# Attention and MLP in one kernel: transposes of the last four half groups moved to DMA, loads two half groups ahead, a new plan

## The chip, the cores and the metric

The kernel runs on one core of a Trainium2 chip. The metric is the device time of one execution in microseconds (us), lower is better. Engines are called as the profile calls them: PE (TensorE matmul), PEld (its weight load), DVE (VectorE), ACT (ScalarE), POOL (GpSimd), SP (SyncE, which here only issues DMAs). A trailing q (SPq) is the part of an engine that issues DMAs and waits.

## What is computed

Inputs are q, k, v and f_logit, each 4 batches x 8 heads x 768 positions x 48, and two MLP weights, 384 x 2048 and 2048 x 384, all float32. Cut to what matters:

```python
f = 1.0 / (1.0 + np.exp(-f_logit))
for t in range(S):
    state = f[:, :, t, :, None] * state + np.einsum('bhd,bhe->bhde', k[:, :, t], v[:, :, t])
    y[:, :, t] = np.einsum('bhd,bhde->bhe', q[:, :, t], state)
x = y.transpose(0, 2, 1, 3).reshape(B * S, H * D)     # 3072 x 384
h = x @ w_in
out = (h * (1.0 / (1.0 + np.exp(-h)))) @ w_out        # 3072 x 384
```

So there is a linear attention with a decay per channel, and then an MLP with a SiLU over every row of its result.

## The kernel before, in words

**Tiling.** Positions go in chunks of 128, so there are six chunks; batches go in two halves of two. A *half group* m (0 to 11) is one chunk of one half; j (0 or 1) is the batch in it. A unit (m, j) is 128 positions of one batch with its 8 heads. m = 0 is loaded and computed in a special way (WIDE), the others alike.

**Tasks.** The work is cut into named tasks; "A8.0" is task A of m = 8, j = 0. For a unit, in the order of their dependence:

- f, k, q, v: the four loads, 192 KB each, issued by SP (load, L250).
- L (ACT): exp and ln of the gate; cs (PE, L314): cumulative sum; ia, aa (ACT): exponentials of it; al, ea: the chunk's total decay.
- ki (POOL, L327) and qg (DVE, L330): k and q scaled by them, in bf16, 64 columns for each head. vb (POOL): v in bf16.
- T (PE, transposes, L363): q and k are turned, eight 128x128 matmuls against an identity into PSUM; qk (DVE, L368) copies them to SBUF.
- A (PE, scores, L386): k times q; am (DVE, masked, L397): causal mask; Y (PE, outputs, L416 and L420): the unit's result; yc (DVE, L435): copied to SBUF in bf16; D and st: the state for m + 2.
- X (PE, turn, L441): three 128x128 transposes of y; xT (DVE, turned, L446) copies them to SBUF.

The MLP of a half group follows: I (PE) multiplies xT by w_in, S (ACT) does the SiLU into hT, O (PE) multiplies hT by w_out, R (ACT, L524) copies the result from PSUM, G stores it. Each is cut in steps: I of a half group has 8 steps of six 128x256 matmuls (mlp_in, L504), or, for m in SPLIT, 8 steps of twelve 128x128 ones (mlp_in_unit, L489), four for each j, so that they can start when one j is there; O has 8 steps of four 128x384 matmuls (mlp_out, L519). A step is named by its first index: I8.4, O7.1.12.

**What sets the order.** Every engine works its instructions in the program's order. A planner (class Plan) makes that order at build time: each task has an engine, an assumed duration, needs, a rank and the buffers that it takes; the planner plays the engines forward with these assumptions and always starts the task that can start first, the lower rank at a tie. MLP steps have ranks from 1000 up, so that attention goes first wherever it is ready. A need on another engine counts as done some time after its end (DRAIN: 0.24 for PE, 2.0 for a load), and for PE tasks of m >= 3 another 0.8 is added (spare), in the planner's units of a us. Where PE would have nothing, fillers (warm, L535: a matmul of zeros) are put in. The planner's durations are assumptions and no measurement; on the chip each engine simply waits at an instruction whose input isn't there.

**Loads.** The pool of load buffers has 8 for each of f, k, q, v, that is four half groups; the load of m waits until the task that reads the buffer of m - 4 is done. All loads, and the stores of m >= 8 (LATE), are issued by SP, in one order.

Of the kernel before, what the change touches and what calls it, by code (L numbers as in the profile page):

```python
# [11 lines left out]
F32 = mybir.dt.float32  # L12
# [6 lines left out]
class Plan:  # L19
# [14 lines left out]
    def add(self, name, engine, us, emit=None, needs=(), rank=0.0, takes=None, frees=None, table=None, opens=0,  # L34
            silus=0):

        m = int(name.lstrip(string.ascii_letters).split(".")[0] or 0)
        spare = self.spare if engine == "PE" and m >= 3 else 0.0
        self.tasks[name] = dict(name=name, engine=engine, us=us, emit=emit, needs=list(needs), rank=rank,
                                takes=[takes] if isinstance(takes, str) else takes or [], frees=frees, table=table, opens=opens, silus=silus, spare=spare)  # L40

    def transfers(self):

        queues = [[n for n, t in self.tasks.items() if t["engine"] == e] for e in ("LD", "WT")]
        left = {n: self.tasks[n]["us"] for q in queues for n in q}
        now = 0.0
        self.lands = {}
        while any(queues):
            heads = [q[0] if q and self.issued[q[0]] <= now else None for q in queues]
            if not any(heads):  # L50
                now = min(self.issued[q[0]] for q in queues if q)
                continue
            rates = self.SHARE if all(heads) else [1.0 if h else 0.0 for h in heads]
            step = min(left[h] / r for h, r in zip(heads, rates) if h)
            later = [self.issued[q[0]] - now for q, h in zip(queues, heads) if q and not h]
            step = min([step] + later)
            now += step
            for q, h, r in zip(queues, heads, rates):
                if h:
                    left[h] -= step * r  # L60
                    if left[h] < 1e-6:
                        self.lands[h] = now
                        q.pop(0)
# [14 lines left out]
    def run(self, filler=None):  # L78
# [6 lines left out]
        left = dict(tasks)  # L85
        for t in tasks.values():
            for n in t["needs"]:
                assert n in tasks, (t["name"], n)
        self.silus = self.ins = self.exps = turned = 0
        while left:  # L90
            best = None
            fronts = {}
            for t in left.values():
                ready = 0.0
                for n in t["needs"]:
                    if n not in end:
                        ready = None
                        break
                    ready = max(ready, end[n] + (self.DRAIN.get(tasks[n]["engine"], 0.1) + t["spare"]) * (tasks[n]["engine"] != t["engine"]))
                if ready is None:  # L100
                    continue
                p = self.pool_ready(t, end)
                if p is None:
                    continue
                e = t["engine"]
                start = max(ready, p, free.get(e, 0.0))
                swap = t["table"] is not None and table is not None and t["table"] != table
                fronts.setdefault(e, []).append((start, swap, t))
            for e, cands in fronts.items():
                cands = [c for c in cands if self.allowed(c, fronts, free)]  # L110
                if not cands:
                    continue
                first = min(s for s, _, _ in cands)
                now = [c for c in cands if c[0] <= first + 1e-6]
                choice = min(now, key=lambda c: c[2]["rank"])
                if best is None or choice[0] < best[0]:
                    best = choice
# [8 lines left out]
            if e in ("LD", "WT"):  # L126

                self.issued[t["name"]] = start
                free[e] = start
                end[t["name"]] = max(start + t["us"], self.lands.get(t["name"], 0.0))  # L130
                self.log.append((start, end[t["name"]], e, t["name"]))
                if t["emit"] is not None:
                    self.order.append((start, t["emit"]))
                del left[t["name"]]
                continue
# [33 lines left out]
            del left[t["name"]]  # L169
# [21 lines left out]
    spare = 0.8  # L191

# [6 lines left out]
def kernel(  # L199
# [10 lines left out]
    nc = tc.nc  # L210
# [7 lines left out]
    NT = d_ff // 128  # L218
    HB = B // 2
# [4 lines left out]
    ld = ctx.enter_context(tc.tile_pool(name="ld", bufs=8))  # L224
# [5 lines left out]

    WIDE = (0,)
# [22 lines left out]
    qg = [singles.tile([C, HB, H, 64], BF16, name=f"qg{i}") for i in range(4)]  # L254
    ki = [singles.tile([C, HB, H, 64], BF16, name=f"ki{i}") for i in range(4)]
# [102 lines left out]

    def transposes(m, j):
        t = tps.tile([128, 2, NP, C], BF16, name="t_ps")  # L360
        for i, src in ((0, qg), (1, ki)):
            for p in range(NP):
                nc.tensor.transpose(t[:, i, p, :], src[m % 4][:, j, 2 * p:2 * p + 2, :], ident)  # L363
        t_ps[m, j] = t

    def transposed(m, j):
        qkT[m, j] = wk.tile([128, 2, NP, C], BF16, name="qk", bufs=3)
        nc.vector.tensor_copy(qkT[m, j], t_ps[m, j])  # L368
# [56 lines left out]
    def output_copy(m, j):  # L425
        if m in WIDE:
            if j == 0:
                both = wk.tile([C, HB, HD], BF16, name="yw")
                for a in range(2):
                    ysb[m, a] = both[:, a]  # L430
                ysb[m] = both
# [83 lines left out]
    def mlp_out(m, j, n):  # L515
        if n == 0:
            os[m, j] = hps.tile([C, d_model], F32, name="o_ps", tag="h_ps")
        for i in range(n, n + 4):
            nc.tensor.matmul(os[m, j], hT[m][:, i, j * C:(j + 1) * C], w_out_sb[:, i, :],  # L519
                             start=(i == 0), stop=(i == NT - 1))  # L520

    def result(m, j):
        osb[m, j] = wk.tile([C, d_model], F32, name="o_sb", bufs=4)
        nc.scalar.copy(osb[m, j], os[m, j])  # L524

    def store(m, j):
# [3 lines left out]
        eng.dma_start(out=out[r0:r0 + C, :], in_=osb[m, j])  # L530
# [8 lines left out]
    plan = Plan({"yd": 2, "t": 1, "a": 1, "h": 3, "qk": 3, "atm": 2, "y": 2, "ia": 4, "aa": 4,  # L539
# [3 lines left out]
    def do(fn, *args):  # L543
# [3 lines left out]
    W = dict(m=8, j=3, L=0, cs=0, ia=-15, aa=1, ki=4, qg=1, vb=-8, T=7, qk=1, A=7, am=-2, Y=11,  # L547
             yc=1, D=25, st=-3, X=4, xT=-9, al=-4, ea=3, va=13)
    LATE = 8
    SPLIT = (1, 2, 3)  # L550
# [6 lines left out]
    for m in range(NH):  # L557
        for j, name in [(j, x) for x in "fkqv" for j in range(HB)] if m in WIDE else [(j, x) for j in range(HB) for x in "fkqv"]:
            user = U({"f": "L", "k": "ki", "q": "qg", "v": "vb"}[name], m - 4, j)
            first = (m, j, name) == (0, 0, "f")  # L560
            add(U(name, m, j), "LD", (0.85 if m in WIDE else 1.07) + 1.5 * first,
                None if m in WIDE else do(load, m, j, name), [user] if m >= 5 else [])

    add("issues", "ACT", 4.5, None, rank=-1e9)
    for m in range(NH):
# [3 lines left out]
        for j in range(HB):  # L569
# [16 lines left out]
            if wide:  # L586
# [3 lines left out]
            add(n("T"), "PE", 0.45, do(transposes, m, j), [n("qg"), n("ki")], rank=base + W["T"], takes="t")  # L590
            add(n("qk"), "DVE", 0.7, do(transposed, m, j), [n("T")], rank=base + W["qk"], takes="qk", frees=[n("T")])
            add(n("A"), "PE", 0.34, do(scores, m, j), [n("qk")], rank=base + W["A"], takes="a")
            add(n("am"), "DVE", 1.32, do(masked, m, j), [n("A")], rank=base + W["am"], takes="atm", frees=[n("A")])
            add(n("Y"), "PE", 0.45 if wide else 0.38, do(outputs, m, j), [n("am"), n("vb")] + ([n("va")] if wide else []) + olds,
                rank=base + W["Y"], takes="yd", frees=[n("qk"), n("am")])
# [5 lines left out]
            add(n("X"), "PE", 0.17, do(turn, m, j), ins("yc"), rank=base + W["X"], takes="yd", frees=[] if wide else [n("yc")])  # L601
            add(n("xT"), "DVE", 0.38, do(turned, m, j), [n("X")], rank=base + W["xT"], frees=[n("X")], takes="xT" if j == 0 else None)

        if m in SPLIT:
            for j in range(HB):
                for n in range(0, NT, 4):
                    add(f"I{m}.{j}.{n}", "PE", 0.68, do(mlp_in_unit, m, j, n),
                        [U("xT", m, j), f"wi{n // 4 * 512}"] + ([f"I{m}.{j}.{n - 4}"] if n else []),
                        rank=1000 + m * 10 + j * 3 + n * 0.1, takes=["h", "hT"] if j + n == 0 else "h", silus=4 if n == 0 else 0,
                        frees=[U("xT", m, 0)] if n == NT - 4 and j == HB - 1 else None)  # L610
                    add(f"S{m}.{j}.{n}", "ACT", 0.64, do(silu_unit, m, j, n), [f"I{m}.{j}.{n}"], rank=-1000 + m,
                        table="silu", frees=[f"I{m}.{j}.{n}"])
        else:
            for n in range(0, NT, 2):
                add(f"I{m}.{n}", "PE", 0.655, do(mlp_in, m, n),
                    [U("xT", m, j) for j in range(HB)] + [f"wi{n // 4 * 512}"] + ([f"I{m}.{n - 2}"] if n else []),
                    rank=1000 + m * 10 + n * 0.1, takes=["h", "hT"] if n == 0 else "h", silus=8 if n == 0 else 0,
                    frees=[U("xT", m, 0)] if n == NT - 2 else None)
# [3 lines left out]
        for j in range(HB):  # L622
            for n in range(0, NT, 4):
                add(f"O{m}.{j}.{n}", "PE", 0.655, do(mlp_out, m, j, n),
                    [f"S{m}.{j}.{n}" if m in SPLIT else f"S{m}.{n + 2}", f"wo{n}"] + ([f"O{m}.{j}.{n - 4}"] if n else []),
                    rank=1000 + m * 10 + 5 + j + n * 0.1, takes="h" if n == 0 else None,
                    frees=[owner] if n == NT - 4 and j == HB - 1 else None)
            add(f"R{m}.{j}", "ACT", 0.5, do(result, m, j), [f"O{m}.{j}.{NT - 4}"], rank=-500.0, frees=[f"O{m}.{j}.0"])
            add(f"G{m}.{j}", *(("SP", 0.05) if m >= LATE else ("POOL", 0.85)), do(store, m, j), [f"R{m}.{j}"], rank=-501.0)
            add(f"W{m}.{j}", "DMA", 0.6, None, [f"G{m}.{j}"], rank=-1)  # L630
# [71 lines left out]
```

## Time and profile before

| what | us |
|---|---|
| median of 6 runs (195.17 to 197.25) | 196.48 |
| the profiled execution, own time | 195.17 |
| its span, first to last instruction | 193.4 |
| PE busy | 186.6 |
| of it fillers (L535, 75 of them) | 16.1 |
| DVE, ACT, POOL busy | 111.6, 130.3, 56.9 |
| ACT table loads (14 of 1283 ns) | 18.0 |
| PE busy from 36.0 to 190.2 (154.2 us) | 153.8 |

The page's busy time of PE is from issue to end of pipelined matmuls, so that neighbours overlap; what a group costs PE is read from the distance of starts in the timeline. The idle time of an engine that is not on the chain is no loss.

### The profile page before, as it was taken

The page shows a single profiled execution, that of the slowest core. Times are in us where ns is not written, and L with a number is a line of the kernel's source. Part 1 is how long each engine was busy: PE and PEld are TensorE (multiplying, and loading weights), DVE is VectorE, ACT ScalarE, POOL GpSimd, SP SyncE. Part 2 cuts the span into 40 slices and gives each one's busy share as a digit, 9 for nine tenths or more (in the row PEclk, how much of TensorE's full clock was granted, in tenths as well). Part 3 has the DMA queues.
Part 4 walks back from the last instruction along what each step waited for, and adds up shares of the span by engine and source line. Part 5 has one row for each costly group of instructions (what it writes and reads, how often), then busy time and mean ns, then how long its engine had stood idle before and what let it go on. Part 6 is the DMA issues. An engine that isn't in the chain of part 4 may idle for free.

```text
span 193.4 us, 5153 instructions
## 1 busy us (share of the span) xinstructions
PE 186.6 (96%) x2127; PEld 141.1 (73%) x2127; DVE 111.6 (58%) x222; ACT 130.3 (67%) x244; POOL 56.9 (29%) x84
## 2 busy tenths in 40 slices
PE   7889999999999999999999999999999999999993
PEld 3457677998666687878688688976688679886561
DVE  6088875651057993877378989726887883000000
ACT  2764567678865489898989995799775027993111
POOL 7253990010367334241562332007720000000000
PEclk9999999999999999999999999999999999999999
DMA  4998999999999999999989897301120020000222
GB/s 110 222 205 176 184 195 191 184 185 176 215 228 259 208 214 196 218 208 211 218 214 217 179 247 164 69 0 41 51 75 3 0 81 3 0 3 0 81 81 81
DMA packets 101654, 27.06 MB, mean 140 GB/s; under 512 B 96256, under 2 KB 100864, under 8 KB 101632
## 3 DMA queue, kind: packets, MB, share of 16 engines
q1 hardware_dynamic: 94784, 19.67, 51.5%
q0 software_dynamic: 4736, 6.29, 14.5%
q10 hardware_dynamic: 2112, 0.79, 2.2%
q8 instruction: 16, 0.26, 0.6%
q14 instruction: 6, 0.05, 0.1%
HBM read 25.17 MB, written 4.72 MB: 155 GB/s over the span
## 4 chain that ended last, share of the span: by engine, by line
PE 61%; SPq 24%; DMA 9%; ACT 2%; issue 1%; ACTq 0%
SPq L250 24%; PE o_ps L519 24%; PE h_ps L504 22%; DMA f_ld<-in_f_logit_dram 7%; PE t_ps L363 3%; DMA f_w<-in_f_logit_dram 2%; PE a_ps L386 2%; PE h_ps L489 2%; PE y_ps L416 2%; PE y_ps L420 1%; PE x_ps L441 1%; PE d_ps L460 1%; PE cs L314 1%; PE al_ps L351 1%; ACT L287 1%
## 5 line engine op out<-in xcount | busy, mean ns | idle before, releaser
L519 PE MATMUL o_ps<-w_out_sb,hT 128*128 128x384 bf16 x384 | 68.6, 326 | 0.0
L504 PE MATMUL h_ps<-xT,w_in_sb 128*128 128x256 bf16 x432 | 52.1, 273 | 0.4 <-DMA w_in_sb<-in_moe_w_in_dram 0.4
L519 PEld LDWEIGHTS <-hT 128*128 128x128 bf16 x384 | 36.2, 98 | 21.3
L513 ACT ACTIVATE hT<-h_ps 128x512 bf16<-128x512 f32 x72 | 42.5, 597 | 12.0 <-PE h_ps L504 9.5
L504 PEld LDWEIGHTS <-w_in_sb 128*128 128x128 bf16 x432 | 40.5, 98 | 5.8 <-DMA w_in_sb<-in_moe_w_in_dram 0.6
L397 DVE TENSOR_TENSOR atm<-a_ps,triu 128x512 bf16<-128x512 f32 x44 | 28.3, 686 | 4.3 <-PE a_ps L386 4.1
L327 POOL TENSOR_TENSOR ki<-k_ld,ia 128x384 bf16<-128x384 f32 x22 | 22.6, 1032 | 24.0 <-ACT ia L319 21.3
L330 DVE TENSOR_TENSOR qg<-q_ld,a 128x384 bf16<-128x384 f32 x22 | 18.4, 843 | 19.2 <-ACT a L324 19.0
L524 ACT COPY o_sb<-o_ps 128x384 f32<-128x384 f32 x24 | 11.5, 477 | 23.5 <-PE o_ps L519 23.3
L336 POOL CAST vb<-v_ld 128x384 bf16<-128x384 f32 x22 | 12.5, 570 | 46.9 <-DMA v_ld<-in_v_dram 38.1
L368 DVE COPY qk<-t_ps 128x1024 bf16<-128x1024 bf16 x24 | 16.5, 686 | 5.7 <-PE t_ps L363 5.6
L287 ACT ACT_TABLE_LOAD x14 | 18.0, 1283 | 1.8 <-PEq L686 1.6
L489 PE MATMUL h_ps<-xT,w_in_sb 128*128 128x128 bf16 x288 | 18.5, 219 | 0.3 <-ACT hT L497 0.3
L435 DVE CAST y<-y_ps 128x384 bf16<-128x384 f32 x22 | 12.2, 554 | 9.5 <-PE y_ps L420 9.5
L489 PEld LDWEIGHTS <-w_in_sb 128*128 128x128 bf16 x288 | 16.6, 98 | 1.0 <-issue 0.4
L535 PE MATMUL w_ps<-zeros 128*128 128x384 bf16 x75 | 16.1, 360 | 1.2 <-DVE zeros L643 1.2
L497 ACT ACTIVATE hT<-h_ps 128x512 bf16<-128x512 f32 x24 | 13.8, 597 | 3.5 <-PE h_ps L489 2.8
L301 ACT ACTIVATE f_ld<-f_ld 128x384 f32<-128x384 f32 x22 | 11.6, 525 | 5.6 <-DMA f_ld<-in_f_logit_dram 5.5
L319 ACT ACTIVATE ia<-cs 128x384 f32<-128x384 f32 x24 | 11.5, 486 | 4.2 <-PE cs L314 3.5
L535 PEld LDWEIGHTS <-zeros 128*128 128x128 bf16 x75 | 7.7, 106 | 6.4 <-issue 2.2
L480 DVE TENSOR_TENSOR states<-sd,al 48x192 bf16<-48x192 f32 x32 | 11.8, 369 | 0.8
L530 POOL DMA_DIRECT2D out_dram<-o_sb x16 | 9.3, 582 | 9.3 <-ACT o_sb L524 6.6
(76 smaller groups left out, 201.4 us busy)
## 6 DMA issues: line engine op xcount, KB each, us to landing
f_ld<-in_f_logit_dram SPq DMA_DIRECT2D x22, 192.0 KB, 4.5
k_ld<-in_k_dram SPq DMA_DIRECT2D x22, 192.0 KB, 4.5
q_ld<-in_q_dram SPq DMA_DIRECT2D x22, 192.0 KB, 4.0
v_ld<-in_v_dram SPq DMA_DIRECT2D x22, 192.0 KB, 4.1
out_dram<-o_sb POOLq DMA_DIRECT2D x16, 192.0 KB, 3.6
w_in_sb<-in_moe_w_in_dram POOLq DMA_DIRECT2D x4, 384.0 KB, 9.1
w_out_sb<-in_moe_w_out_dram POOLq DMA_DIRECT2D x4, 384.0 KB, 16.8
out_dram<-o_sb SPq DMA_DIRECT2D x8, 192.0 KB, 1.9
```

The lines of the kernel that those rows point to most:

```text
L250: nc.sync.dma_start(out=t, in_=src)
L287: nc.scalar.preload_act_table_set(tables[name])
L327: nc.gpsimd.tensor_mul(slots(m, ki[m % 4][:, j, :, 0:D]), flip(m, loaded[m, j, "k"]), slots(m, ias[m, j]))
L330: nc.vector.tensor_mul(slots(m, qg[m % 4][:, j, :, 0:D]), flip(m, loaded[m, j, "q"]), slots(m, aas[m, j]))
L368: nc.vector.tensor_copy(qkT[m, j], t_ps[m, j])
L397: nc.vector.tensor_mul(atm[m, j][:, r], att[m, j][:, r], triu[:, None, :].to_broadcast([C, NP, C]))
L489: nc.tensor.matmul(h_ps[:, i], w_in_sb[:, kk, (n + i) * 128:(n + i + 1) * 128], xT[m][:, kk, j], start=(kk == 0), stop=(kk == KT - 1))
L497: nc.scalar.activation(hT[m][:, n:n + 4, j * C:(j + 1) * C], hs[m, j, n], AF.Silu)
L504: nc.tensor.matmul(h_ps[:, i], w_in_sb[:, kk, (n + i) * 128:(n + i + 1) * 128], xT[m][:, kk].rearrange("p b c -> p (b c)"), start=(kk == 0 ...
L513: nc.scalar.activation(hT[m][:, n:n + 2, :], hs[m, n], AF.Silu)
L519: nc.tensor.matmul(os[m, j], hT[m][:, i, j * C:(j + 1) * C], w_out_sb[:, i, :], start=(i == 0), stop=(i == NT - 1))
L535: nc.tensor.matmul(w_ps[:, 0:NP * 2 * D], zeros[:, 0:128], zeros, start=True, stop=True)
```

## The change

What it does, part by part:

- **XBAR = 8.** For m = 8 to 11, T is no longer eight matmuls and a DVE copy, but one DMA transpose from SBUF to SBUF on SP's queue (128 x 1024 bf16, 256 KB; q and k lie in one tile for it). X is likewise one DMA transpose of 128 x 384 bf16 (96 KB) in place of three matmuls and a DVE copy. So 8 + 8 DMA transposes are added to SP's queue. In the plan T is given 1.6 and X 0.9, and a need on either adds the 2.0 of a load. The pool of turned q and k has 4 buffers (QK), before 3.
- **AHEAD = 2.** Four load buffers for each name; the load of m waits for the reader of m - 2.
- **SPLIT = (2,)**, before (1, 2, 3): I of m = 1 and m = 3 has 96 matmuls of 128x256 in place of 192 of 128x128.
- **The last result in halves.** O of (11, 1) is done for columns 0 to 191 and then for 192 to 383, each with its own copy R and store G: 32 matmuls of 128x192 in place of 16 of 128x384.
- **The plan.** Other ranks (W), the spare of 0.8 only for PE tasks of m >= 5, and an equal rank is settled by place. Transfers are planned in order of issue.

```diff
-        spare = self.spare if engine == "PE" and m >= 3 else 0.0
+        spare = self.spare if engine == "PE" and m >= self.spare_from else 0.0
...
+    spare_from = 5
...
+    AHEAD = 2
...
-    ld = ctx.enter_context(tc.tile_pool(name="ld", bufs=8))
+    ld = ctx.enter_context(tc.tile_pool(name="ld", bufs=2 * AHEAD))
...
+    XBAR = 8
+    QK = 4
...
-    qg = [singles.tile([C, HB, H, 64], BF16, name=f"qg{i}") for i in range(4)]
-    ki = [singles.tile([C, HB, H, 64], BF16, name=f"ki{i}") for i in range(4)]
+    both = [singles.tile([C, HB, 2, H, 64], BF16, name=f"qgki{i}") for i in range(4)]
+    qg = [t[:, :, 0] for t in both]
+    ki = [t[:, :, 1] for t in both]
...
+    def transposes_dma(m, j):
+        qkT[m, j] = wk.tile([128, 2, NP, C], BF16, name="qk", bufs=QK)
+        nc.sync.dma_start(out=qkT[m, j].rearrange("p x n c -> p (x n) c"),
+                          in_=both[m % 4][:, j].rearrange("p x h d -> p (x h d)"), transpose=True)
+
+    def turn_dma(m, j):
+        if m not in xT:
+            xT[m] = wk.tile([128, KT, HB, C], BF16, name="xT", bufs=4)
+        nc.sync.dma_start(out=xT[m][:, :, j, :], in_=ysb[m, j], transpose=True)
...
-    SPLIT = (1, 2, 3)
+    SPLIT = (2,)
...
-            user = U({"f": "L", "k": "ki", "q": "qg", "v": "vb"}[name], m - 4, j)
+            user = U({"f": "L", "k": "ki", "q": "qg", "v": "vb"}[name], m - AHEAD, j)
...
+            if m >= XBAR:
+                add(n("T"), "LD", 1.6, do(transposes_dma, m, j), [n("qg"), n("ki")], rank=base + W["T"], takes="qk")
...
+            if m >= XBAR:
+                add(n("X"), "LD", 0.9, do(turn_dma, m, j), [n("yc")], rank=base + W["X"], frees=[n("yc")],
+                    takes="xT" if j == 0 else None)
...
+            parts = [(0, d_model)] if (m, j) != (NH - 1, HB - 1) else [(0, d_model // 2), (d_model // 2, d_model)]
```

The built program then has, in numbers: 88 transposes fewer on PE (64 of T, 24 of X), 8 qk and 8 xT copies fewer on DVE, 10 table loads on ACT (before 14), 74 fillers (before 75). Up to the first O step the order on PE is the one of before, but for single places and the two I's that are no longer split.

The end of SP's order, from the last loads on:

```
k10.0 q10.0 T8.0 k10.1 q10.1 T8.1 q11.0 k11.0 T9.0 X8.0 k11.1 q11.1 T9.1 T10.0 T10.1 X8.1
T11.0 X9.0 T11.1 X9.1 X10.0 X10.1 X11.0 G8.0 G8.1 X11.1 G9.0 ... G11.1(first half) G11.1(second half)
```

PE's order from the place where T9.1 is issued in the plan to A11.1, and what follows:

```
O6.1.8 O6.1.12 O7.0.0 al11 Y8.1 O7.0.4 cs11.0 O7.0.8 O7.1.0 Y9.0 D8.1 A9.1 O7.0.12 D9.0 O7.1.4 O7.1.8 cs11.1
O7.1.12 I8.0 I8.2 A10.0 I8.4 Y9.1 D9.1 I8.6 A10.1 I8.8 I8.10 Y10.0 I8.12 A11.0 I8.14 Y10.1 O8.0.0 A11.1
O8.0.4 Y11.0 O8.0.8 O8.1.0 O8.0.12 Y11.1 O8.1.4 O8.1.8 O8.1.12 I9.0 ... I9.14 I10.0 ... I10.14 I11.0 ... O11.1.12
```

## The prediction, made before the changed kernel ran

> **What bounds the kernel now.** First the page: the busy shares, the slices, the chain.
>
> ```profile
> PE 186.6 (96%) x2127; PEld 141.1 (73%) x2127; DVE 111.6 (58%) x222; ACT 130.3 (67%) x244; POOL 56.9 (29%) x84
> ...
> PE   7889999999999999999999999999999999999993
> ...
> DVE  6088875651057993877378989726887883000000
> ...
> PEclk9999999999999999999999999999999999999999
> DMA  4998999999999999999989897301120020000222
> ...
> PE 61%; SPq 24%; DMA 9%; ACT 2%; issue 1%; ACTq 0%
> ```
>
> Two resources are full: DMA up to slice 23 (some 115 us), PE to the end, at full clock. The chain goes through SPq and DMA early and through PE later. Which counts is seen from where PE has fillers: by the windows of L535, 74 of 75 lie before 30 us, and one at 75.65. So loads limit only the first 36 us. The table of windows, for the rest (window, then PE busy, PEld, DVE, ACT, POOL, clock, DMA share, GB/s):
>
> ```profile
> 36.00:190.20 154.20, 153.80 (x1767) 118.56 (x1765) 86.92 (x160) 109.70 (x205) 38.18 (x53) 1.00 0.61 131
> 112.00:163.00 51.00, 51.00 (x604) 40.23 (x603) 37.51 (x68) 33.60 (x64) 11.12 (x14) 1.00 0.26 67
> 163.00:190.20 27.20, 27.09 (x203) 19.46 (x201) 0.36 (x1) 13.34 (x25) 0.00 (x0) 1.00 0.10 37
> ```
>
> PE loses 0.4 us in 154, on true work. From 112 to 163, where the last half groups' attention is, DMA is at 0.26: the transposes go to an idle resource. After 163 there is MLP alone. So what is taken off PE comes off the end, as long as nothing else makes PE wait.
>
> **What comes off PE.** The group's mean (219 ns for a 128x128) is a latency; the cost is the distance of starts, in the timeline (start, length):
>
> ```profile
> 134.72 0.39 PE L363 MATMUL t_ps<-ident,qg 128*128 128x128 bf16 x4
> 134.94 0.39 PE L363 MATMUL t_ps<-ident,ki 128*128 128x128 bf16 x4
> 135.16 0.81 PE L519 MATMUL o_ps<-w_out_sb,hT 128*128 128x384 bf16 x4
> ...
> 144.67 0.33 PE L441 MATMUL x_ps<-ident,y 128*128 128x128 bf16 x3
> 144.84 2.13 PE L504 MATMUL h_ps<-xT,w_in_sb 128*128 128x256 bf16 x18
> 146.80 0.21 PE L416 MATMUL y_ps<-states,qk 128*128 128x96 bf16 x1
> ```
>
> - T takes 135.16 - 134.72 = 0.44 us; eight go: 3.5 us.
> - X takes 0.17 us; eight go: 1.4 us.
> - The two unsplit I's: an L504 step is (146.80 - 144.84) / 3 = 0.65 us, an L489 step 0.67 (36.59 to 37.26). 16 steps: 0.3 us less. They now wait for both j; the earlier O and I steps cover it, and the fillers, 74 against 75, say that no new hole is planned.
> - Halves of the last result: 32 matmuls of 192 columns stream as many columns as 16 of 384; 192 columns are 0.08 us (starts 6.94 to 7.02), above the 0.056 of a 128x128, so weight loads stay hidden: 0. Behind the last matmul stand a copy and a store. The copy is 477 ns for 384 columns and 597 for 512, so some 0.30 for 192: 0.2 us less. The store lands in 1.9 us; half the bytes save perhaps 0.1 more. Together 0.3.
>
> Sum 3.5 + 1.4 + 0.3 + 0.3 = 5.5 us.
>
> Off the path: DVE loses 8 x 0.686 + 8 x 0.354 = 8.3 us, ACT four table loads of 1283 ns, 5.1 us. Neither ends PE's wait today, so both count as nothing. Were ACT or DVE the bound somewhere, it would help.
>
> **What is added: 16 transposes on SP's queue.** The trace shows none, so bounds. Nearest rows:
>
> ```profile
> q1 hardware_dynamic: 94784, 19.67, 51.5%
> ...
> k_ld<-in_k_dram SPq DMA_DIRECT2D x22, 192.0 KB, 4.5
> ...
> out_dram<-o_sb SPq DMA_DIRECT2D x8, 192.0 KB, 1.9
> ```
>
> SP's queue moved 19.67 MB in 51.5% of 193.4 us, 5.06 us per MB; by this a T (256 KB, 0.262 MB) holds the engines 1.33 us and an X (96 KB) 0.50. A store takes 1.9 us to land, of which 1.0 is transfer, so 0.9 is added at the end. A lone T would be there in some 2.2 us. Issue holds SP 0.33 us (store) to 0.6 (the quickest loads); in a quiet queue neither is the limit.
>
> Here the Trainium skill speaks against the change. "VectorE: DVE Perf Modes", section "The three transpose paths", prices a 128x128 at 390 ns on TensorE and 1309 on the DMA crossbar, and its rules prefer TensorE where PSUM will do as destination. Eight blocks one after another would make a T of 10.5 us. But the same table's 390 ns stands against 56 ns from start to start here: it prices a lone transpose. Scaled likewise, 1309 is 190 ns per block, a T of 1.5 us (an estimate). "DMA: Bandwidth & Descriptors", section "Latency and other measured facts", gives DMA transposes 261 GB/s, a T of 1.0 us. The ends are 1.0 and 10.5; I take 1.33, the row's, as its short packets also lie in SP's queue.
>
> Does it fit? The tightest stretch in the built order: SP issues T9.1, T10.0, T10.1, X8.1, T11.0, X9.0, T11.1, five T and two X, which is 5.75 T, plus 0.9 to land. From T9.1's place to A11.1, PE has 19 MLP steps of 0.65 (12.4 us), five Y of 0.38, three A of 0.33, three D and two cs of 0.17 and one al of 0.2 (3.9 us): 16.3 us. With T at 1.33 the last is there after 8.5. The first, T8.0, has two loads (2 x 1.0) ahead of it in the queue and six MLP steps and five small tasks, some 5.2 us, until A8.0: 2.0 + 2.2, it just fits. T9.1 has 5.2 us for 2.2. T11.1 alone, released by Y9.1, has 5.4 us.
>
> New waits on SP: T waits for qg and ki, behind it stand loads of m = 10 and 11; X8.0 waits for yc8.0, behind it k11.1, q11.1 and T9.1, for which A9.1 waits; but Y8.0 lies 20 MLP steps (13 us) ahead of A9.1. G8.1 waits for R8.1, behind it X11.1, which I11.0 needs: some 14 I steps, 9 us, cover it. Removing PE's X takes nothing from the path behind: after Y11.1 come the rest of O8, I9 and I10, over 11 us, before X11.1 is needed.
>
> **Loads two ahead.** They cost no bytes; the window is half. In the plan f10.0 is issued after L8.0 and needed by L10.0, with four O steps and some seven small tasks between: 2.6 + 2.0 = 4.6 us, against the 4.5 that a load takes to land (3.4 to 5.4 late in the trace). So ACT may wait there up to 0.8 us, in each half group perhaps, and behind it on ACT stand exponentials and copies R. Below nothing: with fewer loads in flight, they may land sooner (1.9 as the quiet store). PE has three PSUM buffers for h and sees only part. Without the spare for m = 3 and 4, some A or Y stand 0.8 sooner in the plan and can hold PE by tenths. For both together I allow 1.0 us, with 0 and 4 as ends.
>
> Forecast: 5.5 - 1.0 = 4.5 us less. On the profiled execution (span 193.4, 1.8 around it, 195.17) that is 190.7. The median of the runs lies 1.3 above it: 196.48 - 4.5 = 192.0.
>
> **Rivals.**
>
> 1. Transposes hold the queue (slower). If they don't overlap as loads do, and each holds the queue for what a load takes to land, 4.5 us, the stretch above takes 5.75 x 4.5 + 0.9 = 26.8 us against 16.3: PE stalls 10.5 us at A10.1, A11.0, A11.1. Net 5.0 slower: 201.5. It decides from 5.75 T + 0.9 - 16.3 = 5.5, a T of 3.6 us; stalls begin at 2.7. For it: no row shows a transpose, and the page's 1309 ns per block. Against: the bytes, and 16 engines at 0.26. At 10.5 us per T it would be 45 us of stall, some 236; I give that almost no weight.
>
> 2. The gain is eaten by loads (about the same). Half the window makes ACT wait in each of eight half groups for some 0.5 us, PE with it: 4 us in place of 1.0, so 1.5 us less than before: 195.0; with the spare gone, 196. For it: DMA is full to 115 us today, and the 4.6 against 4.5. Against: PE saw 0.4 us of waits while ACT waited 5.5 us for f in all; a half group's loads are 8 x 1.0 us in the 12 us that PE needs for it.
>
> 3. The change takes nothing off the end since PE waits elsewhere (fillers in the first 36 us grow, as weights and loads mix in another way). Up to the first O step the orders agree nearly, so at most a us either way; it lies within the range of the likeliest.
>
> **Chances.** Likeliest 0.64: 192.0, own range 190.4 (no loss) to 194.5 (3 us lost), half a us at each end for the spread of the runs. Rival 2: 0.13, 194.5 to 197.5. Rival 1: 0.23, from 197.5 up. Of rival 1 the part up to 198.5 is needed to leave out no more than 2 in 10: range 190.3 to 198.5. 0.5%, about what a measurement of this kernel can tell from no change, is 1.0 us. Faster 0.66, within 0.10, slower 0.24.
>
> **What would show it.** Right: PE's windows from 36 us to the end again without idle time; L363 with 128 matmuls and L441's with 48; T landing in under 3 us in the table of DMA issues; no A waiting for DMA; DVE's busy time near 103; the last copy near 0.3. Wrong: PE or PEld of the scores waiting for qk by DMA in the list of waits (rival 1), above all at A8.0, A9.1, A10.1, A11.0, A11.1; ACT's exp waiting for f_ld more than 5.5 us, with PE idle at h_ps or o_ps (rival 2); idle time or fillers of PE beyond those of today in the first 36 us (rival 3). The forecast fails if a T takes over 2.7 us of the queue, or a load lands later than 5 us in the bunches of exponentials.

## The result and the profile after

The changed kernel takes 194.16 us in the median of 35 runs, beside 195.53 of the kernel before in 72 runs on the same chips. Medians here and below are of all runs, while the ratios leave out runs that came out slow (here 5 of the 35). The ratio is 0.9918, 95% interval 0.9903 to 0.9934: a gain of 1.6 us, where 4.5 were forecast. The forecast of 192.0 us stood on a median of 196.48 from six runs; from 195.53, 4.5 us less would be 191.0. The profiled execution of the changed kernel took 193.13 us, with a span of 191.4 (before 195.17 and 193.4), so the profiles differ by 2.0 us and can be compared.

First the page of the kernel after: busy shares, slices, DMA queue of SP, shares of the chain.

```profile
PE 181.6 (95%) x1958; PEld 135.1 (71%) x1958; DVE 105.5 (55%) x206; ACT 125.8 (66%) x241; POOL 55.3 (29%) x84
...
PE   7789989999999999999999999999959999999992
...
DVE  6088867552079889859855589634968810000000
...
PEclk9999999999999999999999999999999999999999
DMA  5999999999999999999997999704983322000222
...
q1 hardware_dynamic: 106704, 22.55, 62.7%
...
PE 74%; DMA 13%; issue 3%; DVE 3%; POOL 2%; ACT 2%; SPq 1%; ACTq 0%; DVEq 0%; POOLq 0%
```

PE has lost 5.0 us of busy time, close to the 5.2 of work in the sum, but a digit of its slices falls to 5 at slice 29, some 140 us. The windows of the kernel after, in the columns of those shown of before (window, PE, PEld, DVE, ACT, POOL, clock, DMA share, GB/s):

```profile
36.00:188.20 152.20, 149.41 (x1619) 113.14 (x1616) 81.06 (x144) 105.40 (x202) 36.70 (x53) 1.00 0.75 152
112.00:163.00 51.00, 49.04 (x532) 36.98 (x531) 30.85 (x53) 33.51 (x62) 10.98 (x15) 1.00 0.61 117
163.00:188.20 25.20, 25.01 (x198) 18.64 (x196) 0.00 (x0) 11.96 (x23) 0.00 (x0) 1.00 0.12 43
```

From 36 us on, PE is idle for 2.8 us, before for 0.4. Most of it lies between 112 and 163, where DMA's share has gone from 0.26 to 0.61. PE's timeline names the place; the bracket is the idle time ahead and what ended it:

```profile
139.45 0.81 PE L549 MATMUL o_ps<-w_out_sb,hT 128*128 128x384 bf16 x4
142.22 1.05 PE L533 MATMUL h_ps<-xT,w_in_sb 128*128 128x256 bf16 x8 [1.96 <-DMA xT<-y]
```

This is I8.0, the first MLP step of m = 8. The O step ahead takes 0.65, so PE could start at 140.1; it starts at 142.2, when X8.1 lands. SP's queue of DMA issues at that time (start, time held):

```profile
131.50 0.53 SPq L269 DMA_DIRECT2D q_ld<-in_q_dram  x1
132.13 1.60 SPq L381 DMA_TRANSPOSE qk<-qgki  x1
135.09 2.82 SPq L381 DMA_TRANSPOSE qk<-qgki  x2
138.01 2.04 SPq L387 DMA_TRANSPOSE xT<-y  x1
140.21 1.29 SPq L381 DMA_TRANSPOSE qk<-qgki  x1
```

The first row of transposes is T9.1. The next is T10.0 and T10.1, which hold SP from 135.09 to 137.91. The copy of y that X8.1 reads is DVE's:

```profile
135.32 0.54 DVE L464 CAST y<-y_ps 128x384 bf16<-128x384 f32 x1
```

It was done at 135.86. So X8.1 stood in line for 2.1 us, held SP for 2.0, and landed 2.2 later. The medians from issue to landing in this kernel are:

```profile
qk<-qgki SPq DMA_TRANSPOSE x8, 4.3
xT<-y SPq DMA_TRANSPOSE x8, 2.8
```

The balance of the two profiles, with a gap counted as the distance of starts above the usual one: work off PE -5.2; gaps of PE from 12.0 to 15.1 us, +3.1 (2.1 at I8.0, 0.6 at Y5.1 behind a DVE copy, 0.6 for weights, and small ones). The 0.6 for weights is a difference: I0.0 and I0.4 wait 1.2 between 26 and 30 us, where before a later step waited 0.6 at 32.58. To this comes the tail, from the start of the last copy to the end: 3.2 before and 3.3 after, +0.1. The sum is -2.0.

### The profile page after: what moved, and what is told of

It reads as the page before. It is cut to its first block, busy times and chain, and to the rows that moved or that the text cites. A ratio compares the mean times of both kernels' runs of the same rounds, so it can differ in the third digit from the quotient of the medians.

```text
span 191.4 us, 4858 instructions
## 1 busy us (share of the span) xinstructions
PE 181.6 (95%) x1958; PEld 135.1 (71%) x1958; DVE 105.5 (55%) x206; ACT 125.8 (66%) x241; POOL 55.3 (29%) x84
## 4 chain that ended last, share of the span: by engine, by line
PE 74%; DMA 13%; issue 3%; DVE 3%; POOL 2%; ACT 2%; SPq 1%; ACTq 0%; DVEq 0%; POOLq 0%
PE h_ps L533 29%; PE o_ps L549 29%; DMA w_in_sb<-in_moe_w_in_dram 4%; DMA q_w<-in_q_dram 3%; PE a_ps L416 3%; PE h_ps L518 3%; DMA f_ld<-in_f_logit_dram 3%; PE t_ps L393 3%; DMA xT<-y 2%; DVE qgki L350 2%; PE y_ps L450 2%; PE y_ps L446 2%; PE cs L334 2%; PE d_ps L489 1%; POOL qgki L347 1%
## 5 line engine op out<-in xcount | busy, mean ns | idle before, releaser
L549 PE MATMUL o_ps<-w_out_sb,hT 128*128 128x384 bf16 (+1 forms) x400 | 68.8, 320 | 0.0
L533 PE MATMUL h_ps<-xT,w_in_sb 128*128 128x256 bf16 x528 | 63.0, 273 | 2.8 <-DMA xT<-y 2.0
L533 PEld LDWEIGHTS <-w_in_sb 128*128 128x128 bf16 x528 | 49.7, 98 | 10.0 <-DMA xT<-y 2.3
L347 POOL TENSOR_TENSOR qgki<-k_ld,ia 128x384 bf16<-128x384 f32 x22 | 22.0, 1003 | 27.7 <-ACT ia L339 26.1
L350 DVE TENSOR_TENSOR qgki<-q_ld,a 128x384 bf16<-128x384 f32 x22 | 19.3, 883 | 14.1 <-ACT a L344 13.8
L555 ACT COPY o_sb<-o_ps 128x384 f32<-128x384 f32 (+1 forms) x25 | 11.6, 463 | 23.5 <-PE o_ps L549 23.4
L398 DVE COPY qk<-t_ps 128x1024 bf16<-128x1024 bf16 x16 | 11.0, 685 | 6.2 <-PE t_ps L393 6.1
L322 ACT ACTIVATE lf<-f_ld 128x384 bf16<-128x384 f32 x22 | 11.5, 523 | 0.7
L344 ACT ACTIVATE a<-cs 128x384 f32<-128x384 f32 x24 | 11.4, 489 | 0.0
L450 PE MATMUL y_ps<-vb,atm 128*128 128x48 bf16 x176 | 10.5, 183 | 0.0
## 6 DMA issues: line engine op xcount, KB each, us to landing
f_ld<-in_f_logit_dram SPq DMA_DIRECT2D x22, 192.0 KB, 4.1
k_ld<-in_k_dram SPq DMA_DIRECT2D x22, 192.0 KB, 4.0
q_ld<-in_q_dram SPq DMA_DIRECT2D x22, 192.0 KB, 4.1
v_ld<-in_v_dram SPq DMA_DIRECT2D x22, 192.0 KB, 4.1
out_dram<-o_sb POOLq DMA_DIRECT2D x16, 192.0 KB, 3.4
out_dram<-o_sb SPq DMA_DIRECT2D x7, 192.0 KB, 1.9
```

The costliest lines, as they stand in the source:

```text
L347: nc.gpsimd.tensor_mul(slots(m, ki[m % 4][:, j, :, 0:D]), flip(m, loaded[m, j, "k"]), slots(m, ias[m, j]))
L350: nc.vector.tensor_mul(slots(m, qg[m % 4][:, j, :, 0:D]), flip(m, loaded[m, j, "q"]), slots(m, aas[m, j]))
L450: nc.tensor.matmul(y_ps[:, 2 * p + r, :], atm[m, j][:, r, p, :], vb[m % 4][:, j, 2 * p + r, :], start=not opened, stop=True, skip_group_ch ...
L533: nc.tensor.matmul(h_ps[:, i], w_in_sb[:, kk, (n + i) * 128:(n + i + 1) * 128], xT[m][:, kk].rearrange("p b c -> p (b c)"), start=(kk == 0 ...
L549: nc.tensor.matmul(os[m, j, cols][:, lo:hi], hT[m][:, i, j * C:(j + 1) * C], w_out_sb[:, i, lo:hi], start=(i == 0), stop=(i == NT - 1))
```

## The experiments

Ratios are to the kernel before, in runs on the same chip, with 95% intervals. Code cuts show only the lines that matter; `...` stands for what is left out.

### The place of X8.1 in the queue

SP's order is the only thing changed, in one place: X8.1 goes ahead of T10.1.

```diff
             plan.transfers()
+        at = {t["emit"]: n for n, t in plan.tasks.items()}
+        when = {at.get(fn): s for s, fn in plan.order}
+        for name, ahead_of in [('X8.1', 'T10.1')]:
+            plan.order = [(when[ahead_of] - 1e-6 if at.get(fn) == name else s, fn) for s, fn in plan.order]
```

> One change against the changed kernel: on SP's queue X8.1 stands before T10.1 instead of behind it; every other engine's order is the same. Theory (place in the queue): in the changed kernel PE waits 2.1 us before I8.0 for X8.1, which SP issues only at 138.01 though its input is there at 135.9, because T10.0 and T10.1 hold SP from 135.09. With the swap X8.1 is issued some 1.5 us or more sooner and lands before I8.0 is due (140.1): the wait falls under 0.3 us and the time by 1.8 to 2.1 us, to some 192.2, ratio to before 0.981 to 0.984. Rival (landing): X8.1's 4.2 us from issue to landing are spent behind the data of T10.0, or T10.1 now comes late for A10.1; then the wait shrinks little or moves, and the time falls by less than 0.7 us.

Measured: 191.97 us, 0.9818 [0.9769, 0.9867]. SP and PE in this kernel:

```profile
132.03 4.27 SPq L381 DMA_TRANSPOSE qk<-qgki  x2
136.39 1.21 SPq L387 DMA_TRANSPOSE xT<-y  x1
137.70 2.86 SPq L381 DMA_TRANSPOSE qk<-qgki  x2
```

```profile
139.35 0.81 PE L549 MATMUL o_ps<-w_out_sb,hT 128*128 128x384 bf16 x4
140.24 0.94 PE L533 MATMUL h_ps<-xT,w_in_sb 128*128 128x256 bf16 x7
```

X8.1 is issued 1.6 us sooner and holds SP for 1.21 in place of 2.04. PE's gap at I8.0 goes from 2.12 to 0.24, and the time falls by 2.0 us, by the ratios as by the two profiles (193.13 and 191.12). Up to T8.0 these two run alike: the last T on PE starts at 105.76 in one and 105.66 in the other. So the gap at I8.0 accounts for all but 0.1 of the difference. One place in a queue was worth somewhat more than the change had brought. This version has the lowest time of all that were measured.

The opposite, each T issued a second time into a spare tile (the copy is read by nothing):

```diff
+        nc.sync.dma_start(out=spare_qk[:, :, j], in_=both[m % 4][:, j].rearrange("p x h d -> p (x h d)"), transpose=True)
```

> The changed kernel with every T issued twice, the second into a tile that nobody reads; all other engines' orders are the same. Theory (what stands ahead of X8.1 on SP's queue sets the wait before I8.0): three more T stand ahead of it, at 1.3 to 1.9 us each, so the wait grows from 2.1 to 6 to 8 us, or the same amount falls partly on A9.1, A10.1 and A11.1; 4 to 7 us slower than the changed kernel, ratio to before 1.012 to 1.028. Rival (the wait is X8.1's own landing, DMA has room): under 1.5 us slower than the changed kernel, ratio under 1.000.

Measured: 204.04 us, 1.0404 [1.0344, 1.0463], beyond what was expected. Two rows of PE's waits (us in total, times, longest):

```profile
PE h_ps L533 <- DMA xT<-y: 5.8, 1, 5.8
PE a_ps L416 <- DMA qk<-qgki: 2.8, 3, 1.5
```

The wait at I8.0 grows most. Earlier in the run A8.0, A9.0 and A9.1, which did not wait in the changed kernel, wait too. Two more gaps of its profile, 2.1 at the weights and 1.4 near 11 us, have nothing to do with T; so the size of this run is not a clean price of eight T.

### Other durations in the plan, and X on PE

The plan was given T 1.9 and X 1.2 in place of 1.6 and 0.9, and the order followed from that.

```diff
-                add(n("T"), "LD", 1.6, do(transposes_dma, m, j), ...
+                add(n("T"), "LD", 1.9, do(transposes_dma, m, j), ...
-                add(n("X"), "LD", 0.9, do(turn_dma, m, j), ...
+                add(n("X"), "LD", 1.2, do(turn_dma, m, j), ...
```

> The changed kernel, planned with 1.9 for T and 1.2 for X in place of 1.6 and 0.9, nothing else; orders differ only in the last half groups, X8.1 stands before T10.0. Theory (the plan's too low costs made the bad place): the wait before I8.0 goes, time 1.5 to 2.1 us under the changed kernel, ratio to before 0.981 to 0.985. Rival (transposes land late wherever they stand): another wait of 1 to 3 us for DMA at an A or an I, no gain.

Measured: 192.59 us, 0.9843 [0.9799, 0.9887]. The wait at I8.0 is gone, and one of 0.9 us is new at A9.1 (PE at the scores, for qk by DMA):

```profile
PE a_ps L416 <- DMA qk<-qgki: 0.9, 1, 0.9
```

Then X of m = 8 to 11 on PE again, T by DMA, planned anew (every other test of X by DMA is changed to XX likewise):

```diff
+    XX = 12
...
-            if m >= XBAR:
+            if m >= XX:
                 add(n("X"), "LD", 0.9, do(turn_dma, m, j), ...
```

> The changed kernel with X on PE and DVE again for all half groups, T by DMA for m = 8 to 11; planned anew, so the orders differ. Theory (place in the queue): X costs PE 8 x 0.165 = 1.3 us again, the wait of 2.1 us before I8.0 goes: 0.8 us under the changed kernel, ratio to before 0.986 to 0.990. Rival (T's landing of 4.3 us is the cost): PE waits for qk at an A, and the time is 1 us over the changed kernel's or more, ratio 0.995 and up.

Measured: 193.81 us, 0.9894 [0.9846, 0.9942]. X by DMA saves PE 1.4 us and brings the wait of 2.1, so that the time with X on PE is about the same (the intervals overlap). X is worth doing by DMA only if its place in the queue is right.

### The price of a transpose by itself

A kernel that only issues DMAs from SP and stores zeros (nothing of the attention or the MLP is computed): 32 T, 32 X, four T each reading the one before, four such X, 16 loads, 24 stores.

> No attention and no MLP: zeros are stored as output, and on an otherwise idle core SP issues 32 T (128 x 1024) back to back, 32 X (128 x 384) back to back, then a chain of 4 T and one of 4 X, each reading what the one before wrote, then 16 loads of 192 KB, then the stores. Its total time says nothing; the profile is read. The prediction's numbers: a T every 1.33 us, an X every 0.5, a lone T there in 2.2 us. Other theory (from the changed kernel's trace, where SP is held at least 1.23 us by a T and 1.18 by an X, and SP's queue needed 20.4 us more for the sixteen): SP's issue sets an X to 1.2 us, a T takes 1.3 to 1.9, and a lone T takes 3.1 us to land, a lone X 2.3.

SP's timeline, and the share of the DMA engines in 40 slices of 3.6 us:

```profile
1.42 44.05 SPq L33 DMA_TRANSPOSE dst<-src  x32
45.52 41.49 SPq L36 DMA_TRANSPOSE xs<-src  x32
...
90.18 10.39 SPq L39 DMA_TRANSPOSE dst<-dst  x4
...
104.81 8.13 SPq L42 DMA_TRANSPOSE xs<-xs  x4
```

```profile
DMA  2999999999999433343334435333412299999995
```

A T takes 44.05 / 32 = 1.38 us of the queue with the engines full; the prediction's 1.33 was right. 0.262 MB in 1.38 us is 190 GB/s. The Trainium skill's "DMA: Bandwidth & Descriptors", section "Latency and other measured facts", gives DMA transposes 261 GB/s (with a middle dimension that isn't contiguous), from which 1.0 us is an estimate; the measurement decides. An X takes 1.30 us, not 0.50, while the engines are at three to four tenths. An X in the chain, with nothing else under way, holds SP for 1.18 us too, so SP's issue is the limit and not the bytes. The chains give the time from issue to landing of a lone one:

```profile
dst<-dst SPq DMA_TRANSPOSE x4, 3.0
xs<-xs SPq DMA_TRANSPOSE x4, 2.3
```

### The rest of the change

All of the change but the transposes (planned anew):

```diff
-    XBAR = 8
+    XBAR = 12
```

> The changed kernel with XBAR = 12: no DMA transposes, T and X of all half groups on PE with DVE copies; loads two ahead, new ranks, halves of the last result stay. Theory (the transposes take 5.0 us of work from PE and cost 2.1 us of wait, the rest of the change costs about 1 us of small waits): 2.5 to 3.2 us slower than the changed kernel, so 0.5 to 1.5 us slower than before, ratio to before 1.003 to 1.008. Rival (the rest of the change is free or a gain, and the transposes cost more than the one wait): ratio to before 0.995 to 1.000.

Measured: 197.71 us, 1.0111 [1.0066, 1.0156]: the rest costs 2.2 us, more than either theory had. Three rows of PE's waits in it:

```profile
PE t_ps L393 <- DVE qgki L350: 1.3, 1, 1.3
...
PE t_ps L393 <- DVE qk L398: 1.2, 1, 1.2
PE h_ps L533 <- DMA w_in_sb<-in_moe_w_in_dram: 1.1, 2, 0.8
```

The first is at 10.8 us, at the T of the very first unit, and not at a T of m = 10, as an expectation below has it. PE's order there is that of the changed kernel, which waits 0.2 at this place, while the run with every T doubled, in the same order again, waits 1.3. So this wait differs between executions and is no mark of the missing transposes. The second is at T8.1, where PE's order is another than in the changed kernel. The third is at I0.0 and I0.4.

Its parts were then taken one by one. The last result in one piece, all other orders the same:

```diff
-            parts = [(0, d_model)] if (m, j) != (NH - 1, HB - 1) else [(0, d_model // 2), (d_model // 2, d_model)]
+            parts = [(0, d_model)]
```

> The changed kernel with the last result in one piece, other orders the same. The prediction gave the halves 0.3 us of gain. Profiles of before and after show 3.2 and 3.3 us from the last copy's start to the span's end, so theory now: within 0.3 us of the changed kernel, ratio to before 0.990 to 0.994. Rival: 0.3 us or more slower than the changed kernel, its tail over 3.5 us.

Measured: 194.96 us, 0.9927 [0.9892, 0.9961], beside 0.9918: the halves bring nothing that can be measured, though an interval this wide does not exclude the 0.3 us.

The late work on PE as before, with the ranks, split and spare of before; of the change there are left the loads two ahead, the halves, and the joint tile of q and k with its four buffers:

```diff
-    XBAR = 8
+    XBAR = 12
-    W = dict(m=8, j=6, L=-5, cs=-2, ia=-9, aa=-2, ki=0, qg=6, ...
+    W = dict(m=8, j=3, L=0, cs=0, ia=-15, aa=1, ki=4, qg=1, ...
-    SPLIT = (2,)
+    SPLIT = (1, 2, 3)
-    spare_from = 5
+    spare_from = 3
```

> The late work stays on PE as before, with the ranks, the three split half groups and the spare of before; of the change only the two smallest parts are left: loads two half groups ahead and the last result in halves. The kernel with all of the change but the transposes was 2.2 us slower than before (1.0111). Theory (ranks, split and spare cost these 2.2): 0.997 to 1.003. Rival (the short window of loads costs them): 1.008 to 1.014.

Measured: 199.03 us, 1.0212 [1.0160, 1.0263]. And the same with the new ranks, so that only split and spare are as before:

> As the kernel with all of the change but the transposes, with the split of three half groups and the spare from m = 3 given back; the new ranks stay. Theory: the waits for the weights at I0.0 and I0.4 (0.95 and 0.44) shrink to some 0.5 in all, since the units of I1.0 stand between again, and the wait of 1.3 for qg of m = 10 at T10 stays, as the ranks make it: 1.004 to 1.008. Rival 1 (the ranks make all of it): 1.009 to 1.013. Rival 2 (split and spare make all of it): 0.997 to 1.003.

Measured: 199.05 us, 1.0195 [1.0133, 1.0256]. The expectations of both failed: giving parts of the old plan back made it worse. The wait for the weights at I0.0 did shrink (to 0.3), but 1.4 came at 88.1 at a D, and others.

The transposes alone: XBAR = 8 with four half groups of loads, the whole last result, and the ranks, split and spare of before.

> The transposes alone: T and X of m = 8 to 11 by DMA, with the ranks, split, spare, four half groups of loads and the whole last result of before. In SP's order T8.0, T8.1, T9.0, T9.1, X8.0, X8.1 stand together behind the last load, T10.0 after X8.1. Theory (PE loses 8 x 0.44 + 8 x 0.17 = 4.9 us, and with X8.1 ahead of T10 no new wait comes): 0.973 to 0.981. Rival (the long window makes loads bunch ahead of T8.0, and A8.0 waits some 2 us for it): 0.983 to 0.990.

Measured: 195.07 us, 0.9991 [0.9961, 1.0021]. Neither expected it: PE's busy time is 182.4, so the work is gone, but its gaps are 16.7 us in place of 12.0. Two of them, in PE's timeline:

```profile
87.16 0.62 PE L393 MATMUL t_ps<-ident,qgki 128*128 128x128 bf16 x8 [1.58 <-DVE qgki L350]
...
120.54 0.33 PE L489 MATMUL d_ps<-vb,qgki 128*128 128x96 bf16 x4 [1.56 <-DVE xT L475]
```

The first is at 87 us, long before the first T by DMA is issued. Half the window and the halves added to that:

> As the transposes alone with the ranks, split and spare of before, but loads two half groups ahead and the last result in halves; in SP's order T8.0 and T8.1 stand among the loads of m = 10 and 11, and X8.0 and X8.1 ahead of T10.0. Theory (the short window keeps the queue thin when T8.0 comes; all of 4.9 us is gained): 0.973 to 0.981, and below the run with the transposes alone if that one waits for T8.0. Rival (a loss of 1 to 2 us elsewhere, for loads that come late): 0.981 to 0.988.

Measured: 197.68 us, 1.0107 [1.0058, 1.0156], above both theories and 2.6 slower than the one with the long window. But its order is another too.

All these kernels have orders of their own: beside the kernel before, PE's order is another from 28 or 56 us on. So the parts were tried with every order held. The kernel before with half the load buffers and nothing else:

```diff
-    ld = ctx.enter_context(tc.tile_pool(name="ld", bufs=8))
+    ld = ctx.enter_context(tc.tile_pool(name="ld", bufs=4))
```

> The kernel before with half the load buffers (4 for each name, so loads run two half groups ahead), every order as before. Theory (the window by itself costs nothing; the 4 us of the run with the ranks of before and the short window come from the other order that the plan makes of it): 0.997 to 1.004. Rival (the short window itself makes ACT and POOL, and PE with them, wait for loads): 1.010 to 1.022.

Measured: 195.14 us, 0.9987 [0.9960, 1.0014]. And with the joint tile of q and k and four buffers of turned q and k added, orders of before still:

```diff
-    qg = [singles.tile([C, HB, H, 64], BF16, name=f"qg{i}") for i in range(4)]
-    ki = [singles.tile([C, HB, H, 64], BF16, name=f"ki{i}") for i in range(4)]
+    both = [singles.tile([C, HB, 2, H, 64], BF16, name=f"qgki{i}") for i in range(4)]
+    qg = [t[:, :, 0] for t in both]
+    ki = [t[:, :, 1] for t in both]
...
-        qkT[m, j] = wk.tile([128, 2, NP, C], BF16, name="qk", bufs=3)
+        qkT[m, j] = wk.tile([128, 2, NP, C], BF16, name="qk", bufs=4)
```

> The kernel before with every order as before, half the load buffers (0.9987 alone), q and k of a half group in one tile, and 4 buffers of turned q and k. Theory (these parts are free, and the 2.2 us of the run without the transposes lie in the order that the plan gives): 0.996 to 1.003. Rival (the joint tile makes DVE and POOL slower, and costs the 2.2 us): 1.007 to 1.014.

Measured: 195.50 us, 1.0013 [0.9978, 1.0048]. So neither the short window nor the joint tile costs anything that can be measured by itself. With the halves at nothing too, what is left of the 2.2 us is the order (ranks, split, spare) that the planner gave. This is by elimination: no run shows what the order costs.

The other way round, the order with X8.1 ahead was held, and T and X were done on PE again at the places where their DMAs stood:

```diff
-        nc.sync.dma_start(out=qkT[m, j]..., transpose=True)
+        transposes(m, j)
+        transposed(m, j)
...
-        nc.sync.dma_start(out=xT[m][:, :, j, :], in_=ysb[m, j], transpose=True)
+        turn(m, j)
+        turned(m, j)
```

> As the run with X8.1 ahead of T10.1 (0.9818), but T and X of m = 8 to 11 are done on PE again, with their DVE copies, each at the place in the orders where the DMA transpose stood; nothing is planned anew, all other instructions keep their places. Theory (where the order is held, what leaves PE is worth its whole 4.9 us): 197.0 us, 1.005 to 1.011. Rival (PE would have waited there anyway, and the transposes are worth 2 to 3 us): 0.992 to 0.998.

Measured: 200.20 us, 1.0246 [1.0207, 1.0286], above both theories and 8.2 us above the 191.97. The two profiles differ by 10.1 us: the 4.9 of work, and 5.2 more of gaps. Of these, 1.8 are at the weights, before the first place where the kernels differ, and so don't come from the transposes; the profile is of the slowest of the six runs. The rest is mostly where PE now stands at T, X and D for DVE. So in this order the DMA transposes are worth their 4.9 us of work and more. The whole 8.2 is not their price, as this order was made for T and X by DMA.

### The short window and the queue

The version with X8.1 ahead, with 8 load buffers for each name and every order the same:

```diff
-    ld = ctx.enter_context(tc.tile_pool(name="ld", bufs=2 * AHEAD))
+    ld = ctx.enter_context(tc.tile_pool(name="ld", bufs=8))
```

> The kernel swap with eight load buffers for each name in place of four, all orders the same, so loads can start up to four half groups ahead, as before the change. Theory (the short window costs next to nothing: SP's queue is full until 50 us either way): within 0.7 us of swap, ratio to before 0.979 to 0.985. Rival (the short window makes loads late, and part of the missing 2 us is there): 1 us or more under swap, ratio under 0.977.

Measured: 193.91 us, 0.9899 [0.9857, 0.9942], against 0.9818 [0.9769, 0.9867] with 4; the intervals just overlap. Neither theory had it: the long window is slower, not faster or the same. A row of PE's timeline in this kernel shows a wait that the one with 4 does not have, and SP's rows show the queue at that time:

```profile
120.78 0.40 PE L416 MATMUL a_ps<-qk 48*128 48x128 bf16 x8 [1.95 <-DMA qk<-qgki]
```

```profile
112.75 1.13 SPq L269 DMA_DIRECT2D q_ld<-in_q_dram  x1
114.06 1.98 SPq L381 DMA_TRANSPOSE qk<-qgki  x1
116.09 0.67 SPq L269 DMA_DIRECT2D k_ld<-in_k_dram  x1
116.81 0.84 SPq L269 DMA_DIRECT2D q_ld<-in_q_dram  x1
117.82 3.59 SPq L381 DMA_TRANSPOSE qk<-qgki  x1
```

With 4 buffers T8.0 is issued at 110.79, behind loads that hold SP for 0.4 us; with 8 at 114.06, behind ones of 0.9 to 1.6, and A8.0 waits. That the short window keeps the queue thin when the first T comes is argued from this one pair of profiles and not shown. The one with 8 is of the slowest of its six runs (195.47). It is 4.3 us longer than the one with 4, where the medians differ by 1.9, and 2.1 of the 4.3 lie ahead of T8.0 (the last T on PE starts at 107.79, with 4 at 105.66).

## Why the prediction was right and wrong

**Right: the mechanism and the work.** PE was the bound and is it still. L393 has 128 matmuls, L470 48, PE's busy time is 5.0 us less, and the forecast of T's time on the queue (1.33) is 1.38 measured back to back. Two of its signs did not come: T lands in 4.3 us and not in under 3, and DVE's busy time is 105.5 and not near 103. Rival 1, transposes that hold the queue for 3.6 us, is out. Rival 2, loads that come late, is out too: ACT waits 6.2 us for f in place of 5.5, and in the order of before the short window costs nothing that can be measured.

**Wrong: the step "Does it fit?".** It left out one wait, that of I8.0 for X8.1, and gave X too little time on the queue and to land. It counted the stretch T9.1 to T11.1 for the A's, and it named the A's as the places to watch. None of them waits. X8.1 is in that same list, behind T10.0 and T10.1, and I8.0 needs it; for X only X8.0 and X11.1 were looked at. That wait took 2.1 of the 2.9 us that are missing, and moving the one DMA gave 2.0 back. The prediction's own sizes would have let it pass by 0.9 us: from T10.0's issue at 135.1, two T of 1.33, an X of 0.50 and 0.9 to land is 139.2, and PE needs it at 140.1. The trace has 2.8 for the two T, 2.0 for X and 2.2 to land. So looking at X8.1 would not have been enough; the sizes of X were needed too. (The stretch also has four A and not three, 0.3 us more room, which changes nothing.) That 194.16 lies between 190.4 and 194.5, the range of the likeliest case, says little for the sum, since that range allowed for 3 us lost anywhere.

**Mis-sized terms.** X on the queue: 0.50 from bytes, 1.2 measured (up to 2.5 behind others), since its issue and not its bytes is the limit. A lone T: 2.2 to be there, 3.0 measured, and 3.1 to 5.2 in the kernel. From the end of its hold, X8.1 took 2.2 to land, not 0.9. Halves of the last result: 0.3 hoped for, nothing measured; the copy is shorter by 0.16 and the store lands 0.3 sooner, yet from the last copy's start to the end of the span it is 3.3 us, before 3.2. Why is open.

**The rest of the change.** The working gave +0.6 (split, halves) and an allowance of -1.0, together 0.4 us of loss; without the transposes it is 2.2. The allowance was put on the loads and on the spare. The loads cost nothing in the order of before; by elimination the new order does. "The fillers, 74 against 75, say that no new hole is planned" was read as no new hole, but a plan's hole and the chip's are not the same. Before, the split I1.0.0 stood between I0.2 and I0.4, and a later step waited 0.6 us for weights; now I0.0 and I0.4 wait 1.2. This is rival 3, at 0.6 us in this pair of profiles. Such sizes are not safe: the same T starts at 105.7 us in the version with X8.1 ahead and at 107.3 in the one with T and X on PE again, though every order is the same up to there. That one order is good with the transposes (0.9818) and poor with the same work on PE (1.0246) shows that order and parts cannot be priced apart by adding.

**Still open:** why the planner's orders differ by up to 5 us in PE's gaps is known by places (a DVE copy, a decay that ACT had not done, weights), not by a cause, and part of each profile's gaps differs from one execution to the next.

## What to carry to other kernels

When work is moved to a queue, write down every consumer of every transfer on it, with who stands ahead of it, and not only the consumers of the biggest transfers: here a small one, behind two others, cost more (2.0 us) than the change brought (1.6). Price a small DMA transpose by what it holds its issuer, and not by its bytes. And before parts of a change that share a planner or scheduler are judged one by one, hold the order: replanned runs here came out 2 to 5 us from what the part under test was expected to bring, and no run showed why.

## What the hardware showed that was not expected

- A DMA transpose of 96 KB holds SP for 1.2 us (32 back to back take 1.30 each), nearly as long as one of 256 KB (1.38 each), with the DMA engines at three to four tenths.
- DMA transposes of 256 KB run at 190 GB/s with the engines full (32 back to back), where the stores of 192 KB in the same run reach some 370 GB/s.
- The same transpose lands in 3.0 us in a quiet chain and in 4.3 (median) in the kernel's queue.
